# A new order of issue for the 2,740 hand-listed steps of a DeltaNet and MLP-mixer kernel

## The chip, the cores and the metric

The kernel runs on one core of one Trainium2 chip, in one launch. The time is that of the launch on the device, in microseconds (us); lower is better. A comparison of two kernels uses the medians of their runs.

## What is computed

The reference is a DeltaNet recurrence per batch and head, then an MLP-mixer (first over the tokens, then over the channels), all in float32:

```python
# q, k, v: (4, 8, 768, 48); beta: (4, 8, 768)
k_n = k / (np.linalg.norm(k, axis=-1, keepdims=True) + 1e-06)
state = zeros((B, H, D, D))
for t in range(S):
    kt, vt, bt = (k_n[:, :, t], v[:, :, t], beta[:, :, t, None])
    y[:, :, t] = np.einsum('bhd,bhde->bhe', q[:, :, t], state)
    v_old = np.einsum('bhde,bhd->bhe', state, kt)
    state = state + bt[:, :, :, None] * np.einsum('bhd,bhe->bhde', kt, vt - v_old)
# bridge: (B,H,S,D) -> x of (B, S, H*D) = (4, 768, 384)
xt = x.transpose(0, 2, 1)
h = np.maximum(xt @ w_tok1, 0.0) @ w_tok2      # 768 -> 256 -> 768
u = x + h.transpose(0, 2, 1)
h2 = np.maximum(u @ w_ch1, 0.0) @ w_ch2        # 384 -> 1536 -> 384
return u + h2
```

## The kernel before

The recurrence is done in chunks of 64 tokens. Inside a chunk the 64 updates are written as the inverse of a triangular 64 x 64 matrix, so that the tokens of a chunk are handled by matrix products and only the 48 x 48 state passes from chunk to chunk. There are 12 chunks in each of the 4 batches, so 48 steps of the recurrence, r0 to r47. Two chunks, 128 tokens of one batch with all eight heads, are a unit: 24 units, u = 0 to 23, six to a batch.

Everything is written as small Python generators ("jobs"). A job is called until its next `yield` and issues a few instructions each time; that is a step. The jobs, with the lines that matter here:

- `k{u}`, load_kq: the loads of k and q from HBM into pads (for early units) and kst (L403, four loads of 48 KB). `p{u}`, prep: squares of k (ksq, ScalarE, L465), their sum (VectorE, L468), the norm, the scaling, and the transposes of k and q into kq, by TensorE with a copy by ScalarE (L507, L511) for early units and by VectorE (L368) for units from 12 on.
- `c{u}` and `d{u}`, grams: for the first and the second chunk of a unit, the products of the transposed k with k and q (L442, p_g, two 64 x 128 products to a step), then a masking product on VectorE into gm.
- `t{u}`, to_parts, `i{n}`, invert, and `f{u}`, from_parts: 16 x 16 diagonal blocks are gathered from gm, inverted by VectorE (L655 to L687; seven rounds, i0 to i6) and put back. For the first six units the gathering is done by copies on three engines; for later ones four DMAs of a unit write the blocks to n_dram in HBM (L610), and four read them back (L635).
- `h{u}`, join_16, and `j{u}`, join: the inverses of 16 x 16 blocks are joined to those of 32 x 32 and 64 x 64 (L701 to L722, and L740 to L769: p_z L764, p_x L751).
- `v{u}`, load_v: four loads of v (L403, v_st, two buffers), then two scalings on GpSimd (POOL; L413, L416).
- `r{t}`, recur: one step of the recurrence: p_k (L804) from the state, rest (VectorE, L811), p_y and p_w (L824, L828), the copy w_t (ScalarE, L834), p_s (L842) and p_y (L843), the new state s_t (VectorE, L851 and L853), the output (ScalarE, L856).
- `m{b}`, mixer: the token and channel mixing of batch b in full 128 x 128 products (p L1000, p_h L1013, p_ut L1023, p_c L1080 for batch 0, p_r L972 for the others, p_o L1102, the addition L1031). Batch b's mixer fills TensorE while the recurrence of batch b + 1 goes on; m3 comes last, alone.
- `w{n}`, round_weights: a load of a piece of the mixer's weights into one of three buffers (L273, d64) and its rounding (ScalarE L279, VectorE L282, POOL L286). `s`, sum_weights (L913): sums of weights that the mixers need. `b`, load_beta. `x`, `z`, `Y`: products on zeros, with which TensorE is kept running while it has nothing else.

The matrix products of the recurrence and its preparation have at most 64 rows and 64 columns of the 128 x 128 array. Each uses one quarter of it: a row half (the partitions of its operands) and a column half (the partitions of its output).

The whole order of issue is one string of words, written out in the kernel (from L1176). A word is a job's name and `*n` for n steps in a row. A loop behind it takes them one after another:

```python
    for word in order.split():
        name, _, n = word.partition("*")
        for _ in range(int(n or 1)):
            next(jobs[name])
```

Each engine executes its own instructions in the order in which the string issues them. The DMAs here are issued by SyncE (SP), in order too: a DMA whose source is not ready holds up all those behind it. Buffers of a pool are given out in the order of allocation, so the string also decides which buffer a tile gets and whose last reader it has to wait for.

Of the kernel before, what the change touches and what calls it, by code (L numbers as in the profile page):

```python
# [23 lines left out]
def kernel(  # L24
# [149 lines left out]
    t11 = const.tile([128, NB, HB], FP32, name="t11")  # L174
# [18 lines left out]
    w1 = const.tile([128, NCH, DTOK], FP32, name="w1")  # L193
    w2 = const.tile([128, NDH, S], FP32, name="w2")
# [340 lines left out]
    t16 = spare[:, cuts[1] : cuts[2]].rearrange("s (q t b) -> s q t b", q=2, t=QB)  # L535
# [647 lines left out]
    c4*4 d4*2 w8 w6 i0*2 d4 z v0*2 i0*3 x k8 z*3 w1 i0*2 d4 x w17*3 t4 z h0*4 i0
    k5*2 h1*2 k8 h1*2 h0 h1 w17 z f0*3 h0 w8*2 p3 v1 h0 p5 f1*3 k8 h0*3 v1 v0 h0*2
    v0 h2*3 t4 h2 h0 z f2 h2 w0*2 j0 w11 j0 w6 j0*4 k5 h1*6 j0*3 h1*2 f2*2 j1 p5 t4
    v0 j0*2 w6 p5*6 h2 p5 r0 w14 h2*2 r0*4 h2*4 c5*4 k7 k9 h2 r0*2 p8 p5 j1 c5 j1*2
    r0 k7 r1*2 k7 k9 r1 k9 w0*2 r1 d5*3 r1 k9 w11*3 d5*2 j1 r1 w14 p6*2 w9 p8 v2 j1
    h3*2 t5 j2 r1 p6 h3*2 f3 r1 k9*2 h3 j1*2 w14 j1*3 k7 p6 t5*2 r1*2 r2*3 w9 r2 x
    j2*3 i1*2 w14 j2*2 p6 r2*2 w16 r2 p6 f3*2 h3 i1*4 k10 r2*2 h3 i1 h3 d6 h3 p6 r2
    r3*2 d6 r3 d6 r3 i1 v2 x i1 h3*4 r3 d6 v2*2 w16 c6*2 w9 c6*2 k10 d6 c6 p7 w16  # L1190
    p7 r3 j3 j2*2 r3 p7 r3*2 j2*2 j3 w9 j3 r4*2 k7 v3 p7 r4*2 j2 r3 j3*2 v2 j3 w16
    r4 k10 p7*2 w24 v3 r4*2 k10 i1*2 t6 i1 w5 p7*2 r4 w27 p7 j3*4 r4*2 d7 i1 r5 i1
    r5 i1 r5 j3 k8 v3*2 d7 r5*2 d7*3 k10 w5 c7*3 r5 w27 w5 v4 r5 w5 c7*2 r5 p8*3
    r5*2 r6*4 w24 v4 t7 i1 z p8*4 p9 v3 r6 h5 w27 h5 v4*2 h5*3 r6*2 w26 h4*2 t7 d8
    h4 w24 i1 h4*2 t7 d8*3 r6 w24 w27 t7 c8*4 t6*2 f4*3 d8 h4*3 p9 w26 p9 r6 r7 k10
    r7 r6 h4 p8 c8 w28 t6 h4*3 v4 r7*2 h4 w7 p9 r7 p9*2 r7 p9*2 r7*2 p9 c9 w26 w28
    j4 d9 c9 w26 k11 c9*2 f5 p10 w28*2 d9*3 r7 c9 r8*2 w7 t8*2 d9 r8*2 j4*2 p10 t8
    j4*2 w7 j4 p7 p10 t8 v5 m0 f5 p10 p9 f5 v5 j4*3 w4 w15 w4 r7 t9*2 w4 j4*2 t9*2
    h5 w15 z r8*2 h5*2 v5 h5 v5 r8*2 w27 w7 w4 w15 Y r8 r9*4 h5*3 r8 p10 h5 i2 j5*2
    r9*2 i2 w29 j5 p10*2 r9 j5 i2*3 j5 w29 w12 k11*2 k12 j5 r9 i2 k11 v7 m0 r9 w15  # L1200
    r10 j5*2 i2 j5 w12 w29 r10*2 i2 w19 i2 r10 p10 m0 p10 w19 k11*2 r9 v5 w12*2 k12
    d10*2 i2 w22 j5 d10 j5 r10*2 x i2 d10 i2 r10 w19 Y r10 i2*2 m0 w29 r10 w19 z
    w21 Y p11 k12 r11 r10 w31 Y i2 w22*2 r11*3 k12 i2*2 r11 i2 m0 r11 i2*2 w22 v7*2
    c10 w31 r11*2 c10*2 i2 k12*2 r11 m0 x i2*4 v7 k12 i2*4 x z w25 v6*2 m0 i2*2 v6
    k12*2 v6 k12 i2 f6 m0*2 c10 m0 f6*3 w25 m0 c10 m0 w21 w25*3 f7 m0*2 p11 w21*2
    w23 f7 m0*2 w27 d10 m0 p11 j6 v6 j6*4 p10 f7 w31*2 f7 w30 f8*3 p12 j6 j7 p12
# [92 lines left out]
```

## Time and profile before

| | before |
|---|---|
| median of 3 runs | 648.06 us |
| the runs | 646.71, 648.06, 651.08 us |
| span of the profiled execution, first to last instruction | 645.9 us |
| mean clock granted to TensorE | 0.987 |
| DMA traffic | 50.27 MB, mean 78 GB/s |

No other time of the profiled execution is known than its span. The profile's page lists for each engine its busy time; PE is TensorE's matrix products, PEld its weight loads, which run beside them; DVE is VectorE, ACT ScalarE, POOL GpSimd, SP SyncE. A line such as L842 is a line of the kernel's file. Rows of the waits and of the timeline name an instruction by engine, line, operation, and its tiles as output <- input; in brackets stands the idle time of the engine before it and what ended that. The page's overview over 40 slices of the span (busy share in tenths, granted clock in tenths, DMA rate in GB/s):

```profile
PE   8589888999999999999999999999999999999997
...
DVE  4986866978789756798977998585726353372643
ACT  7759767437412342223632423134326140232240
POOL 2437255224400221002100101010020000000000
PEclk8979979999999999999999999999999999999999
...
GB/s 185 166 126 130 164 147 180 158 104 139 112 88 80 89 105 74 95 89 100 93 71 125 58 78 42 63 17 50 5 44 4 25 3 0 25 1 25 1 26 25
```

One slice is 16.1 us. The costliest lines of the kernel are the full-size products of the mixers:

```profile
L1102 PE MATMUL p_o<-wc,r 128*128 128x192 f32 x720 | 126.3, 329 | 0.9 <-ACT u_t L1027 0.6
...
L1102 PE MATMUL p_o<-wc,s 128*128 128x192 f32 x288 | 51.2, 330 | 0.3 <-DVE xb L1031 0.3
...
L442 PE MATMUL p_g<-kq 48*64 48x128 f32 (+1 forms) x704 | 37.5, 285 | 7.8 <-ACT kq L511 6.2
```

The columns are the line, the engine, the operation with output and inputs, the count, then the busy time in us and the mean length of one in ns, then the idle time of the engine in front of them and what ended most of it.

### The profile page before, as it was taken

How to read it: one execution, taken by the hardware profiler on the slowest of the kernel's cores; microseconds unless marked ns; L12 is line 12 of the kernel's file. 1: busy time of each engine (PE TensorE's matmuls, PEld its weight loads, DVE VectorE, ACT ScalarE, POOL GpSimd, SP SyncE). 2: the span in 40 equal slices, each digit the busy share in tenths (PEclk: the TensorE clock that was granted, in tenths of full speed). 3: DMA queues.
4: the chain of work that ended last, by engine and by line, in shares of the span. 5: the costliest groups of instructions: out<-in, count | busy, mean ns of one | idle time of the engine just before them, and what ended most of it. 6: DMA issues, size and time to landing. Idle time of an engine off the chain costs nothing. (4 is left out here: it accounts for less than half of the span.)

```text
span 645.9 us, 21493 instructions
## 1 busy us (share of the span) xinstructions
PE 615.6 (95%) x9136; PEld 533.2 (83%) x9136; DVE 446.8 (69%) x1132; ACT 259.9 (40%) x631; POOL 109.0 (17%) x147
## 2 busy tenths in 40 slices
PE   8589888999999999999999999999999999999997
PEld 4457766668888987968989999769999987999997
DVE  4986866978789756798977998585726353372643
ACT  7759767437412342223632423134326140232240
POOL 2437255224400221002100101010020000000000
PEclk8979979999999999999999999999999999999999
DMA  9755666545533343344434222202010000000000
GB/s 185 166 126 130 164 147 180 158 104 139 112 88 80 89 105 74 95 89 100 93 71 125 58 78 42 63 17 50 5 44 4 25 3 0 25 1 25 1 26 25
DMA packets 135776, 50.27 MB, mean 78 GB/s; under 512 B 114656, under 2 KB 130144, under 8 KB 135680
## 3 DMA queue, kind: packets, MB, share of 16 engines
q1 hardware_dynamic: 135680, 48.89, 33.3%
q8 instruction: 72, 1.18, 0.8%
q14 instruction: 24, 0.20, 0.1%
HBM read 39.42 MB, written 9.44 MB: 76 GB/s over the span
## 5 line engine op out<-in xcount | busy, mean ns | idle before, releaser
L1102 PE MATMUL p_o<-wc,r 128*128 128x192 f32 x720 | 126.3, 329 | 0.9 <-ACT u_t L1027 0.6
L1102 PEld LDWEIGHTS p_o<-wc,r 128*128 128x128 f32 x720 | 116.7, 190 | 3.0 <-ACT u_t L1027 1.1
L984 DVE TENSOR_TENSOR r<-r,p_r 128x512 f32<-128x512 f32 x90 | 59.4, 684 | 39.1 <-PE p_r L972 36.7
L1031 DVE TENSOR_TENSOR xb<-xb,p_o 128x192 f32<-128x192 f32 x84 | 29.3, 350 | 52.9 <-PE p_o L1102 52.7
L981 ACT COPY r<-p_r 128x512 f32<-128x512 f32 x54 | 31.3, 584 | 85.6 <-PE p_r L972 78.3
L668 DVE TENSOR_TENSOR x<-x,sub 128x84 f32<-128x84 f32 (+24 forms) x178 | 58.9, 331 | 6.1
L663 DVE TENSOR_TENSOR sub<-x 128x84 f32<-128x84 f32 (+24 forms) x178 | 58.0, 326 | 7.4 <-DMA x<-n_dram 3.2
L1080 PE MATMUL p_c<-u_t,wc 128*128 128x256 f32 x216 | 51.3, 387 | 1.3 <-ACT r L1089 0.7
L1102 PE MATMUL p_o<-wc,s 128*128 128x192 f32 x288 | 51.2, 330 | 0.3 <-DVE xb L1031 0.3
L1102 PEld LDWEIGHTS p_o<-wc,s 128*128 128x128 f32 x288 | 46.8, 190 | 1.2 <-DVE xb L1031 0.6
L1080 PEld LDWEIGHTS p_c<-u_t,wc 128*128 128x128 f32 x216 | 39.6, 190 | 7.4 <-ACT r L1089 1.1
L416 POOL TENSOR_TENSOR v_st<-v_st,nrm 128x384 f32<-128x384 f32 x24 | 20.3, 847 | 146.9 <-DMA v_st<-in_v_dram 79.4
L442 PE MATMUL p_g<-kq 48*64 48x128 f32 (+1 forms) x704 | 37.5, 285 | 7.8 <-ACT kq L511 6.2
L988 ACT ACTIVATE r<-r 128x512 f32<-128x512 f32 x54 | 33.8, 631 | 25.4 <-DVE r L984 25.1
L499 POOL TENSOR_TENSOR mb<-mask_c,cs 128x512 f32<-128x512 f32 x20 | 21.0, 1048 | 128.7 <-DVE cs L478 102.6
L856 ACT ACTIVATE xb<-p_y 64x192 f32<-64x192 f32 x96 | 31.1, 324 | 23.8 <-PE p_y L843 16.0
L972 PE MATMUL p_r<-u_t,wc 128*128 128x128 f32 x288 | 38.6, 277 | 0.0
L972 PE MATMUL p_r<-t_d,wc 128*128 128x128 f32 x288 | 37.7, 281 | 0.0
L442 PEld LDWEIGHTS p_g<-kq 48*64 48x64 f32 (+1 forms) x704 | 26.8, 136 | 12.0 <-ACT kq L511 7.3
L834 ACT COPY w_t<-p_w 128x192 f32<-128x192 f32 x48 | 15.2, 318 | 51.6 <-PE p_w L828 50.7
L972 PEld LDWEIGHTS p_r<-u_t,wc 128*128 128x128 f32 x288 | 35.3, 192 | 0.3
L972 PEld LDWEIGHTS p_r<-t_d,wc 128*128 128x128 f32 x288 | 34.1, 191 | 1.1 <-DVE r L984 0.2
(176 smaller groups left out, 1252.8 us busy)
## 6 DMA issues: line engine op xcount, KB each, us to landing
d<-in_moe_w_ch_dram SPq DMA_DIRECT2D x24, 384.0 KB, 3.8
v_st<-in_v_dram SPq DMA_DIRECT2D x96, 48.0 KB, 2.4
out_dram<-xb SPq DMA_DIRECT2D x23, 192.0 KB, 1.9
kst<-in_k_dram SPq DMA_DIRECT2D x64, 48.0 KB, 2.7
n_dram<-gm SPq DMA_DIRECT2D x72, 32.0 KB, 1.8
pads<-in_k_dram SPq DMA_DIRECT2D x24, 96.0 KB, 2.6
pads<-in_q_dram SPq DMA_DIRECT2D x24, 96.0 KB, 3.2
gm<-w_dram SPq DMA_DIRECT2D x72, 32.0 KB, 2.1
```

The lines of the kernel that those rows point to most:

```text
L442: nc.tensor.matmul(p_g[PAR[i ^ cc], p], kqt[f, p, cc, 0], kqt[f, p, cc])
L499: scaler.tensor_tensor(out=mb, in0=mask_c[:, None, None, :].to_broadcast([128, NP, 2, C]), in1=cs[:, :, :, None].to_broadcast([128, NP, 2, ...
L663: nc.vector.tensor_tensor(out=tmp, in0=y[:, :, 0:s, s : s + 1].to_broadcast([n, k, s, w]), in1=y[:, :, s : s + 1, s + 1 : m].to_broadcast( ...
L668: nc.vector.tensor_tensor(out=y[:, :, 0:s, s + 1 : m], in0=y[:, :, 0:s, s + 1 : m], in1=tmp, op=ALU.add,)
L856: nc.scalar.mul(y[:, :, D * i : D * i + D], p_y[PAR[1 - i]], 1.0 if c else -1.0)
L972: nc.tensor.matmul(p[:, i], pieces[i // width][:, at : at + 128], f[f"u{n}"], start=first and i == 0, stop=True, skip_group_check=True,)
L981: nc.scalar.copy(o, p)
L984: nc.vector.tensor_tensor(out=o, in0=o, in1=p, op=ALU.add if sign > 0 else ALU.subtract)
L988: nc.scalar.activation(o, o, ACTF.Relu)
L1031: nc.vector.tensor_tensor(out=xb[:, c, e], in0=xb[:, c, e], in1=p, op=ALU.add)
L1080: nc.tensor.matmul(p_c[:, k], piece_of(wc1, cb, f * 128)[:, f * 128 : (f + 1) * 128], u_t[:, cb], start=(cb == 0), stop=(cb == NCB - 1),)
L1102: nc.tensor.matmul(p, a[:, m], wc2[:, m, j], start=(start and i == 0), stop=(i == NM - 1), skip_group_check=True,)
```

## The change

Only the string `order` is changed. Both strings have 2,740 steps and every name the same number of times, so every job issues the same instructions with the same operands in the same order within the job. How the jobs' steps are interleaved is new from the first line to the last; the new string is broken into 101 lines instead of 85 because it has fewer repetitions (`*n`). It comes from a search with a model fitted on the trace. In the string after the change every line number of the kernel above it is as before; lines below it are 16 higher.

The diff, cut to the start, the grams of u0 to u3, the place where w5, w27, w24 and t6 lie, the loads of k17, and the end:

```diff
     order = """
-    w10 z w10*2 z k1 z b k0 k1*2 b z x k1*2 k3 k0 z k1 k0*2 p1*2 k0 w2 k0 p0*2 b p1
-    p0 w10 p0*7 p1*3 k3*2 w2 d0 w2 c0 k2*2 c0 w18 d0*3 k3 w2 c0*3 d0 k3 p1*3 c1*2
-    p1 c1*3 k2*4 p2 d1 x d1*3 k3 t0 p2*2 w3 d1 p2*2 w13 p2*4 c2*2 d2 p2 p3*2 k4*3
...
-    c3 t2*2 t3*2 k7 p4 w1 t3 i0 p6 i0 p6*2 p4*2 i0*7 k8 z p4*4 v1 c4 k8 w6 d4 w1
...
-    r4 k10 p7*2 w24 v3 r4*2 k10 i1*2 t6 i1 w5 p7*2 r4 w27 p7 j3*4 r4*2 d7 i1 r5 i1
-    r5 i1 r5 j3 k8 v3*2 d7 r5*2 d7*3 k10 w5 c7*3 r5 w27 w5 v4 r5 w5 c7*2 r5 p8*3
...
-    p16 m0 r21*2 j12*2 k16 j12 f13 k17 r21 j12*2 p16 r22*4 m0*2 p15 v11 r22*3 p16
-    m0 k17*2 r22 k17*2 s*3 k17 r22*2 c16 d16 t15 c16 d16 f12 d16*3 c16 t15 r23 c16
-    t14*2 k17*2 r23*4 p17 m0 k17*3 r23 c16 p17*5 k17 p17 m0*4 s c17 v12 d17 c17*2
...
-    m2*2 r45 m2*3 r46*5 m2*5 j23 m2*12 r46*2 m2 r46*3 m2*4 r47*4 m2*4 r47*3 m2*6
-    r47 m2*5 m3*4 r47 m2*2 m3*2 m2 m3*7 m2*12 m3*2 m2 m3*159
+    w10 k1 k0 b k3 k1 w10 k1 k0 z k1*2 z w10 k0 w2 k0 z*2 k0*2 b w10 k2 k1 k3 p0 b
+    x v0 k3 w13 p0*3 p1 z p1 p0*5 p1 x w2 w3 k2 k4 w2 p1*2 d0 c0 d0 c0 d0 c0 v1 k2
+    p0 d0 p1 k2 d0 k2 c0 k2 c0 k4 p1 k5 k3 p1 k3 p1 d1 p2 w2 d1 c1 d1 p1 c1 d1 k3
+    c1 p2 c1 t0 p2 d1 p2*2 p3 c1 p2*2 k4 p2*3 w3 d2 w3 p3 c2 d2 w18 k6 k4 k6 t0
...
+    c3 d3 t1 p4 d3 t2 c3 w13 w1 d3 c3 d3 t1 w18 p4 c3 k5 p4 w18 t2 t3 w8 p4 t0 p6
+    x t3 p4 p6 t3 v1 t2 p4 i0 w1 i0*2 w1 i0 p4 x k5 i0 k6 w18 i0 p6 i0 p4*2 v0 w8
...
+    r3 p7 w5 j2 c6 v2 j2 k10 j3*2 r3 r4*2 p7 j3 i1 r4*3 j2 j3 p7 w16 v3 i1*2 r3 r4
+    v3 w27 i1 j3 p7 w24 p7 i1 p7 t6 r4*2 p7 r4 j3*4 d7 t6 r4 i1*2 r5*4 d7 j3 d7 c7
+    r5 w5 w27 d7 r5 c7 i1 w5 k10 c7 v3 r5 c7 r5 w5 k10 p8 d7 c7 p8 r5 z r6*2 r5
...
+    m0 r22 d16 m0 r22*2 c16 d16*2 s c16 r22 d16 c16 d16 r23 v12 k17 c16 r22 k17
+    p17 f13 k17*2 f12 c16 k17 r23*3 m0 r23 p17 r23 s p17 v12 s t14 p17 t16 v14
...
+    r46 m2*2 r46*2 m2*5 r46 m2*2 r46*2 m2*5 r47*5 m2*11 r47 m2 m3 m2 r47 m3*3
+    r47*2 m3*2 m2 m3*6 m2 m3 m2*4 m3 m2 m3*3 m2*6 m3*157
     """
```

Of the same name every step keeps its number: the first `w5` of the string is always the load, the later ones the rounding.

More of the change, by code (lines that the diff above doesn't have):

```diff
@@ L1183 @@
[L1183 to L1188, printed above, removed]
@@ L1195 @@
[L1195 to L1200, printed above, removed]
@@ L1201 @@
[L1201 to L1206, printed above, removed]
@@ new lines @@
+    w4 t9 j4 h5 p9 r8 w4 w7 p10 t9 h5 t9 w4 r8 t9 h5*2 Y r8 h5*2 w7 k12 p10 j5 r8
+    w15*2 w7 v5 r9 r8 i2*2 h5 i2 r9 i2 w12 r9 w12 r9 m0 r9 i2 p10 r9 j5 w12 j5 r9
+    w15 k11 i2 j5 w19 j5 i2*2 p10 w12 r9 k11 p10 v5 i2 m0 v7 j5 w19 p10 x w29 j5*2
+    k12*2 j5 r9 j5 v7 w29 k11 r10 i2 v5 w22 r9 r10 w29 k12 r10 i2 r10*2 m0 j5 i2
+    w19 r10 p10 w22 i2 r10 i2 Y d10 c10 d10 r10 v7 z r10 r11 Y w19 i2 r11 c10 w22
+    i2 r11 r10 r11*2 m0 i2 r11 k11 w22 d10 p11 r11 v6 Y c10 k12 v6 r11 v6 v7 r11
+    c10 k12 i2 d10 x i2 x i2*2 k12*2 v6 i2*4 w25 i2 m0 w29 m0 i2 m0 i2 w23 w21 i2
```

137 lines of the change are left out of this document (81 added, 56 removed).

## The prediction

> **What bounds the kernel now.** I read the busy line of the page first, then the busy time by stage, then the list of TensorE's waits, and last the timeline around the longest waits. The page:
>
> ```profile
> span 645.9 us, 21493 instructions
> ...
> PE 615.6 (95%) x9136; PEld 533.2 (83%) x9136; DVE 446.8 (69%) x1132; ACT 259.9 (40%) x631; POOL 109.0 (17%) x147
> ```
>
> TensorE (PE) is idle for 645.9 - 615.6 = 30.3 us in all, so nothing on another engine can be worth more than that unless it also makes TensorE's own work shorter. Where the 30.3 us lie is read from the stages; the columns are the stretch, its length, the busy time of each engine with its instructions, the clock granted to TensorE, the DMA share and GB/s:
>
> ```profile
> 0.00:43.00 43.00, 31.56 (x285) 19.65 (x286) 30.95 (x91) 27.87 (x70) 14.69 (x25) 0.88 0.91 172
> 43.00:112.00 69.00, 60.36 (x1714) 50.40 (x1715) 51.19 (x124) 54.75 (x150) 37.57 (x47) 0.95 0.62 146
> 112.00:250.00 138.00, 134.53 (x2193) 110.98 (x2193) 106.25 (x266) 52.88 (x136) 31.10 (x37) 1.00 0.45 108
> 250.00:400.00 150.00, 147.76 (x2265) 132.63 (x2265) 129.24 (x328) 53.80 (x130) 18.91 (x27) 1.00 0.38 85
> 400.00:528.00 128.00, 127.43 (x1924) 113.65 (x1923) 72.90 (x196) 43.37 (x102) 6.71 (x11) 1.00 0.12 27
> 528.00:646.00 118.00, 114.00 (x762) 105.93 (x760) 56.23 (x130) 27.24 (x48) 0.00 (x0) 1.00 0.04 14
> ```
>
> In the first 43 us TensorE lacks 11.4 us and much of its busy time is the filler products on zeros; it waits for loads and for the first inversion. From 43 to 112 us (the recurrence of the first batch, r0 to about r9) it lacks 8.6 us, and the clock of 0.95 costs 60.36 x 0.05 = 3.0 us more. From 112 us on it lacks 3.5 + 2.2 + 0.6 + 3.9 us in 534 us: there the time is TensorE's work, and an order can win only by the few waits left or by packing the products more tightly. Last come the longest waits by cause (total, times, longest):
>
> ```profile
> PE p_g L442 <- ACT kq L511: 6.2, 4, 3.8
> PE p_s L842 <- ACT w_t L834: 3.1, 5, 2.0
> PE p_t L507 <- DMA pads<-in_q_dram: 2.4, 1, 2.4
> PE p_y L843 <- issue: 1.6, 1, 1.6
> PE p_g L442 <- DVE kq L368: 1.5, 1, 1.5
> ```
>
> **The change, part by part.** Both orders have 2,740 steps, the same number of each name, so every engine gets the same instructions (4,652 matmuls, two records each). On TensorE and VectorE an instruction moves on average by under 1 us of its own engine's work, and the first p of m0 (L1000) has the same work ahead of it. So no stage moves as a whole. What moves is the neighbourhood of each step.
>
> *Before 43 us.* The first and third wait (6.2 and 2.4 us) lie here mostly. Their end is set by VectorE's inversion i0:
>
> ```profile
> 29.49 1.95 DVE L655 STREAM_TRANSPOSE x<-r 128x1024 f32<-128x1024 f32 x1
> 42.93 2.06 PE L701 MATMUL p_z<-r,wc 64*64 64x32 f32 x64 [0.40 <-DVE r L679]
> ```
>
> TensorE's next useful product (L701) comes when i0 is through. The new order loads k3, k4 and part of v0 and v1 earlier and moves the reduction of p6 (L468) ahead of i0's transpose; that should take the wait for L511 away, but TensorE would then only wait longer in front of L701. I count 0, from -1 (one step less inside i0) to +2 (a load of u0 to u3 pushed back by v0's).
>
> *From 43 to 112 us.* The 2.0 us wait for w_t is traced to the DMA queue:
>
> ```profile
> 74.33 2.35 SPq L610 DMA_DIRECT2D n_dram<-gm  x1
> 76.77 0.40 SPq L273 DMA_DIRECT2D d<-in_moe_w_tok_dram  x1
> 77.26 0.38 SPq L273 DMA_DIRECT2D d<-in_moe_w_ch_dram  x1
> ...
> 79.95 0.44 ACT L279 ACTIVATE d<-d 128x256 f32<-128x256 f32 x1 [1.05 <-DMA d<-in_moe_w_tok_dram]
> 81.15 0.55 ACT L279 ACTIVATE d<-d 128x384 f32<-128x384 f32 x1 [0.44 <-DMA d<-in_moe_w_ch_dram]
> 82.15 0.32 ACT L834 COPY w_t<-p_w 128x192 f32<-128x192 f32 x1
> 82.52 0.25 PE L842 MATMUL p_s<-w_t,gm 64*64 64x48 f32 x1 [2.01 <-ACT w_t L834]
> ```
>
> SyncE (SP) stood 2.35 us in t6's first write of n_dram, because its block was not ready; the loads of w5 and w27 came behind it, ScalarE waited 1.05 + 0.44 us for them, and the copy w_t of r5, queued behind, came late. In the new order w5, w27 and w24 are issued ahead of t6. ScalarE's queue is unchanged here (both roundings, then w_t), so its work still stands in front, but the 1.49 us of waiting should go: -1.5. That t6 is later costs nothing: its reader, inversion i2, starts far later. After this wait the clock fell:
>
> ```profile
> 83.00:85.00 2.00, 1.92 (x26) 1.42 (x21) 1.60 (x6) 1.23 (x4) 1.43 (x3) 0.54 0.45 83
> 85.00:88.00 3.00, 3.00 (x20) 1.77 (x17) 2.05 (x6) 1.49 (x3) 1.11 (x2) 0.50 0.80 177
> ```
>
> The stretch at about half clock is most of the 3.0 us above, and behind 112 us the stages show 1.00, although waits of 1.6 and 1.5 us lie there. So a wait cut from 2.0 to 0.5 us should not bring it about: I take -3.0, with 0 as the other bound, if the clock falls there all the same. The Trainium skill ("TensorE: Matmul & The Clock Gate", Part 1) says that the clock is either half or full and falls after an idle window of about 3.4 us whose phase runs freely; the 0.50 agrees, the length doesn't: 2.01 us of wait sufficed here. By that rule the remaining 0.5 us could not fill a window either, and the sum would be the same -7.8.
>
> *TensorE's packing.* The recurrence's and the preparation's products use a 64 x 64 quarter of the array each: rows of one half, outputs in the same half ("straight") or the other ("crossed"). A gram step of c is straight, of d crossed; p_z of a join is crossed, p_x straight; p_k is straight in even and crossed in odd steps. The trace shows what the neighbours are worth:
>
> ```profile
> 24.97 0.67 PE L442 MATMUL p_g<-kq 64*64 64x128 f32 x16
> 57.83 1.09 PE L442 MATMUL p_g<-kq 64*64 64x128 f32 x16
> ...
> 63.78 1.12 PE L764 MATMUL p_z<-t,gm 64*64 64x32 f32 x32
> 99.51 0.67 PE L804 MATMUL p_k<-s_t,kq 48*64 48x48 f32 x16
> ...
> 72.76:73.89 1.13, 1.13 (x48) 1.00 0.62 90
> ```
>
> The first sixteen records alternate c and d, the second sixteen are all d: 0.42 us for 8 matmuls, 0.053 us each. A p_z alone takes 1.12 and a p_k alone 0.67 us; where the two were interleaved (last row, 48 records) both took 1.13, so 0.66 us for 24 matmuls, 0.028 us each. I take 0.04. Counted in the two orders, the matmuls that stand in runs of eight or more of one kind fall from 431 to 373 ahead of the first p of m0 and from 385 to 293 behind it. Behind it, where TensorE is the bound: 92 x 0.04 = -3.7, between -2.6 and -4.9. Ahead of it 58 x 0.04 = -2.3, of which half may be lost in waits for the recurrence: -1.2.
>
> Against it stands that the finer order changes more often between full-size and quarter products, 93 times for 89. From the chain of waits:
>
> ```profile
> 517.30 1.98 PE p_r L972 x16
> ...
> 557.72 13.67 PE p_r L972 x120
> ```
>
> 120 in a row take 0.114 us each, so 16 take 1.82; with the change behind them they took 1.98. Four more cost 4 x 0.16 = +0.6, and twice that if the way back costs as much. The Trainium skill ("TensorEngine Tiling (Array Packing)", Key Properties) says that a change of tiling mode drains the engine, which speaks against such an order, and that tiles run independently; the trace agrees with both, at 0.16 us and at 0.42 us for 8 matmuls.
>
> *The wait for L368 at 254 us*, 1.5 us, likewise begins in the DMA queue:
>
> ```profile
> 243.62 2.46 SPq L610 DMA_DIRECT2D n_dram<-gm  x3
> 246.12 1.26 SPq L403 DMA_DIRECT2D kst<-in_k_dram  x2
> 249.84 0.52 ACT L465 ACTIVATE ksq<-kst 128x384 f32<-128x384 f32 x1 [4.04 <-DMA kst<-in_k_dram]
> 252.04 2.02 DVE L368 STREAM_TRANSPOSE kq<-pads 128x512 f32<-128x512 f32 x2
> 254.11 1.15 PE L442 MATMUL p_g<-kq 48*64 48x128 f32 x32 [1.54 <-DVE kq L368]
> ```
>
> The last two loads of unit 17's kst stood behind four writes of n_dram. In the new order the first three of the four stand ahead of one such write, the last behind it. With one write in front instead of four the last load can be about 2 us earlier, and the 1.54 us go: I count -1.0, between -1.5 and 0.
>
> *What the new order adds.* A reordering of 2,740 steps makes waits that this trace cannot show: steps that were late enough for their operands now come earlier. The row nearest is the wait of 2.01 us; I allow one such, +2.0, between 0 (the other engines' queues keep the same work ahead of TensorE's milestones) and three, +6.0.
>
> The sum: 0 - 1.5 - 3.0 - 3.7 - 1.2 + 0.6 - 1.0 + 2.0 = -7.8 us, a span of 638.1. The runs of before were 646.71, 648.06 and 651.08 us, their median 2.2 us above the span; the new time is then 640.3.
>
> **The rivals.** About 1% (6.5 us, outside 641.6 to 654.5) is what a measurement of this kernel can tell from no change.
>
> *Hidden anyway.* The quarter products saved lie under ScalarE's and VectorE's queues: from 43 to 112 us ScalarE is busy for 54.75 and VectorE for 51.19 of 69 us, and from 250 to 400 us VectorE for 129.24 of 150. Then only about half of the packing behind 112 us stays, -1.9, and one of the two DMA waits, -1.3, against +0.6 and +2.0: about 647.5. For it: the orders are near to each other. Against it: after 112 us TensorE lacks only 10 us.
>
> *Slower: w_t behind weight rounding.* ScalarE is in order; a copy w_t behind a rounding whose load is late costs what r5 paid, 2.0 us and a drop of up to 3.0. In the new order the copies of r10 and r11 also stand behind roundings (L279, L280). If each of r5, r10 and r11 paid 5.0 us where before only r5 did, the stage would be 10 us longer; with -3.7 + 0.6 + 2.0 from the rest this gives 657. It decides from two more such events on. Against it: the loads are earlier, not later, in the places I followed.
>
> *Not what it says.* The order also decides which buffer a load gets: v0 is now allocated ahead of v1, and the three d buffers go round in another sequence. A load that waits for a buffer blocks all of SyncE's queue; this would show as the rivals above, without a time of its own.
>
> *Much better.* All waits named go, the clock stays up and nothing new comes: -1.5 - 3.0 - 4.9 - 2.3 - 1.5 + 0.6 = -12.6, about 635.5.
>
> **How the numbers follow.** The forecast's mechanism has 0.58 (0.42 of it below 641.6, the rest between 641.6 and 645), hidden 0.22, much better 0.08, slower 0.12. The second part is the forecast with the clock falling all the same, 640.3 + 3.0 = 643.3. So faster by over 1%: 0.42 + 0.08 = 0.50; within 1%: 0.16 + 0.22 = 0.38; slower: 0.12. The range starts a little under the much better case, at 634. It ends at 651, where the hidden case has nearly its three new waits instead of one (647.5 + 4.0), and leaves out the slower case and an edge of the hidden one, together under 0.2.
>
> **What would show it.** Right: no wait of p_s for w_t near 82 us and no stretch at 0.50 clock after 80 us; L610 no longer ahead of w5 and w27 on SyncE; fewer than 30.3 us of idle; records of L442 and L804 in runs of the shorter kind, and TensorE's busy time down by 3 us or more. Wrong: busy time unchanged (packing was worth nothing), or a new wait over 1.5 us behind 112 us, above all on L368, w_t or rest.

## The result and the profile after

| | before | new order |
|---|---|---|
| median | 648.23 us (4 runs) | 666.89 us (4 runs) |
| runs | 646.71 to 651.08 us | 662.74 to 671.15 us |
| span of the profiled execution | 645.9 us | 660.9 us |
| granted clock, profiled execution | 0.987 | 0.982 |

The new order is slower: the ratio is 1.0318, with a 95% interval of 1.0268 to 1.0369. The prediction was 640.3 us with a range of 634 to 651; it had the sign wrong. The profiled execution is the fastest of the four, so its 15.0 us are the smallest of the runs' losses. The medians of the experiments leave out slow runs (1502 us in e10, 1000 us in e16, three of 650 to 657 us in e11 and e17), and of e10 and e16, whose profiled run was such a one, no profile is read.

The page of the new order:

```profile
span 660.9 us, 21502 instructions
...
PE 618.6 (94%) x9136; PEld 532.2 (81%) x9136; DVE 454.2 (69%) x1132; ACT 260.8 (39%) x631; POOL 110.8 (17%) x147
```

TensorE's busy time is 3.0 us longer and its idle time is 660.9 - 618.6 = 42.3 us instead of 30.3: 12.0 of the 15.0 us are new waits. The 3.0 us of busy time are about the clock: span times (1 - granted clock) is 11.9 us here and 8.4 us before. In the other three runs of the new order the clock was 0.972, 0.976 and 0.981, worth 12.6 to 18.7 us; in 13 runs of before beside the first experiments it was 0.984 to 0.995, worth 3 to 10 us. So of about 19 us in the median some 12 are waits and some 7 are lost clock (a run's time less its lost clock has a median of 652.2 us here and of 639.4 in those 13 runs).

The stages of the new order up to 400 us, with the same columns as in the prediction:

```profile
0.00:43.00 43.00, 29.13 (x280) 17.48 (x281) 32.69 (x89) 27.69 (x70) 14.93 (x27) 0.88 0.85 165
43.00:112.00 69.00, 60.35 (x1699) 48.60 (x1698) 53.04 (x126) 54.89 (x148) 36.24 (x44) 0.98 0.64 149
112.00:250.00 138.00, 130.11 (x2135) 106.68 (x2134) 105.16 (x259) 52.91 (x135) 31.78 (x38) 0.99 0.47 107
250.00:400.00 150.00, 142.41 (x2152) 125.77 (x2144) 119.87 (x306) 48.56 (x119) 18.62 (x24) 0.98 0.36 78
```

From 112 to 250 us TensorE now lacks 7.9 us (3.5 before) and from 250 to 400 us 7.6 us (2.2 before), with the clock at 0.99 and 0.98 where it was 1.00. These are the stages of which the prediction said that "the time is TensorE's work". The stage from 43 to 112 us, where it looked for most of the gain, has the same busy time as before and a better clock, 0.98 for 0.95.

Where the time went is seen best at equal work. The first p_k (L804) of a recurrence step has nearly the same products ahead of it on TensorE in both orders (up to r33, 1.4 us more or less at the steps shown). Its start, in us from the start of the span, read from the timelines:

| step | before | new order | later by |
|---|---|---|---|
| r1 | 57.23 | 58.61 | +1.4 |
| r13 | 152.84 | 152.73 | -0.1 |
| r18 | 201.61 | 204.03 | +2.4 |
| r23 | 245.76 | 250.55 | +4.8 |
| r27 | 298.69 | 306.63 | +7.9 |
| r29 | 311.62 | 323.38 | +11.8 |
| r33 | 352.54 | 366.72 | +14.2 |
| r47 | 519.21 | 536.03 | +16.8 (here some 2 us more work stand ahead of it) |
| end | 645.86 | 660.87 | +15.0 |

Against this execution of the kernel before, the head is not slower; all is lost between r13 and r33, most of it from r23 to r29. But the kernel before had itself lost some time ahead of r13 in this execution, which it does not in most others; that is shown under e7. The largest waits of TensorE in the new order (total, times, longest):

```profile
PE p_g L442 <- ACT kq L511: 6.9, 3, 5.0
PE p_o L1102 <- DVE xb L1031: 4.5, 4, 2.2
PE p_s L842 <- ACT w_t L834: 3.1, 6, 1.0
...
PE p_g L442 <- DVE kq L368: 2.3, 1, 2.3
```

The 2.0 us wait for w_t is gone (longest 1.0). New are the 4.5 us for the addition L1031, which were 0.5 before. Two of these waits, 2.3 us for L368 and 2.2 us for L1031, are longer than 1.5 us and lie behind 112 us: that is the prediction's own sign of being wrong. The timeline shows one of them, with SyncE and VectorE around it:

```profile
267.34 0.34 SPq L657 DMA_DIRECT2D x<-n_dram  x1
...
270.74 0.19 DVE L663 TENSOR_TENSOR sub<-x 128x30 f32<-128x30 f32 x1 [5.26 <-DMA x<-n_dram]
271.58 0.35 DVE L1031 TENSOR_TENSOR xb<-xb,p_o 128x192 f32<-128x192 f32 x1
271.98 2.22 PE L1102 MATMUL p_o<-wc,s 128*128 128x192 f32 x12 [2.16 <-DVE xb L1031]
...
281.28 0.36 SPq L1034 DMA_DIRECT2D out_dram<-xb  x1
```

The load of i4's blocks (L657) left SyncE at 267.34 us; in the old order it left at 260.53 us, though the new order is only 5 us late there. VectorE reached the first step of i4 (L663) and stood 5.26 us until the load landed. The addition that frees TensorE's PSUM buffer was queued behind it, so TensorE waited 2.16 us. Some 38 us later the first p_z of j14, which needs what i4 computed, waited 1.00 us for L740 and that for the read of w_dram, and the clock fell:

```profile
309.78 0.45 DVE L740 STREAM_TRANSPOSE t<-gm 128x256 f32<-128x256 f32 x1 [2.07 <-DMA gm<-w_dram]
...
310.28 0.30 PE L764 MATMUL p_z<-t,gm 64*64 64x32 f32 x2 [1.00 <-DVE t L740]
```

```profile
308.00:312.00 4.00, 2.65 (x67) 2.38 (x66) 2.22 (x4) 0.74 (x2) 0.00 (x0) 1.00 0.53 96
312.00:316.00 4.00, 3.79 (x69) 3.43 (x68) 2.10 (x5) 2.03 (x6) 2.99 (x3) 0.54 0.47 85
316.00:318.00 2.00, 2.00 (x79) 1.94 (x77) 1.19 (x4) 0.07 (x1) 0.00 (x0) 0.50 0.53 128
318.00:320.00 2.00, 2.00 (x14) 2.00 (x14) 1.97 (x4) 1.82 (x5) 0.00 (x0) 0.72 0.26 45
```

This wait and one of 0.35 us right behind it were followed by 8 us at about half clock, worth 4 x 0.46 + 2 x 0.50 + 2 x 0.28 = 3.4 us. The drop cost more than the waits.

### The profile page after: what moved, and what is told of

The parts are those of the page before. It is cut to its first block, busy times and chain, and to the rows that moved or that the text cites. A ratio compares the mean times of both kernels' runs of the same rounds, so it can differ in the third digit from the quotient of the medians.

```text
span 660.9 us, 21502 instructions
## 1 busy us (share of the span) xinstructions
PE 618.6 (94%) x9136; PEld 532.2 (81%) x9136; DVE 454.2 (69%) x1132; ACT 260.8 (39%) x631; POOL 110.8 (17%) x147
## 4 chain that ended last, share of the span: by engine, by line
PE 53%; DVE 15%; DMA 11%; SPq 8%; issue 8%; ACT 3%; POOL 1%; DVEq 0%; ACTq 0%; POOLq 0%
PE p_o L1102 17%; PE p_r L972 15%; DVE x L668 3%; DVE sub L663 3%; SPq L403 3%; PE p L1000 3%; PE p_c L1080 3%; PE p_h L1013 2%; DMA d<-in_moe_w_ch_dram 2%; PE p_k L804 2%; SPq L610 2%; SPq L635 2%; PE p_s L842 2%; DMA w_dram<-x 2%; PE p_y L824 2%
## 5 line engine op out<-in xcount | busy, mean ns | idle before, releaser
L1102 PE MATMUL p_o<-wc,r 128*128 128x192 f32 x720 | 129.4, 332 | 2.7 <-DVE xb L1031 2.1
L1031 DVE TENSOR_TENSOR xb<-xb,p_o 128x192 f32<-128x192 f32 x84 | 29.4, 350 | 61.2 <-PE p_o L1102 61.0
L981 ACT COPY r<-p_r 128x512 f32<-128x512 f32 x54 | 31.6, 585 | 99.2 <-PE p_r L972 99.1
L663 DVE TENSOR_TENSOR sub<-x 128x84 f32<-128x84 f32 (+24 forms) x178 | 59.5, 334 | 15.5 <-DMA x<-n_dram 11.9
L668 DVE TENSOR_TENSOR x<-x,sub 128x84 f32<-128x84 f32 (+24 forms) x178 | 65.7, 369 | 6.1
L442 PE MATMUL p_g<-kq 48*64 48x128 f32 (+1 forms) x704 | 38.9, 284 | 9.5 <-ACT kq L511 6.9
L856 ACT ACTIVATE xb<-p_y 64x192 f32<-64x192 f32 x96 | 31.1, 324 | 37.3 <-PE p_y L843 18.1
L972 PE MATMUL p_r<-t_d,wc 128*128 128x128 f32 x288 | 39.1, 288 | 0.0
L442 PEld LDWEIGHTS p_g<-kq 48*64 48x64 f32 (+1 forms) x704 | 26.6, 136 | 14.5 <-ACT kq L511 7.6
L972 PEld LDWEIGHTS p_r<-t_d,wc 128*128 128x128 f32 x288 | 35.5, 198 | 0.9
L286 POOL TENSOR_TENSOR wc<-w_f,d 128x384 uint32<-128x384 uint32 x24 | 26.0, 1086 | 60.8 <-ACT d L280 14.6
```

The lines of the kernel that those rows point to most:

```text
L286: nc.gpsimd.tensor_tensor(out=dst.bitcast(U32), in0=f, in1=lo, op=ALU.add)
L442: nc.tensor.matmul(p_g[PAR[i ^ cc], p], kqt[f, p, cc, 0], kqt[f, p, cc])
L663: nc.vector.tensor_tensor(out=tmp, in0=y[:, :, 0:s, s : s + 1].to_broadcast([n, k, s, w]), in1=y[:, :, s : s + 1, s + 1 : m].to_broadcast( ...
L668: nc.vector.tensor_tensor(out=y[:, :, 0:s, s + 1 : m], in0=y[:, :, 0:s, s + 1 : m], in1=tmp, op=ALU.add,)
L856: nc.scalar.mul(y[:, :, D * i : D * i + D], p_y[PAR[1 - i]], 1.0 if c else -1.0)
L972: nc.tensor.matmul(p[:, i], pieces[i // width][:, at : at + 128], f[f"u{n}"], start=first and i == 0, stop=True, skip_group_check=True,)
```

## The experiments

Each experiment ran beside kernels before on the same chip; their median was 645.8 to 647.3 us. A ratio is to those, with its 95% interval. The edits of the order are cut to the words where two strings begin to differ.

### Which half: the head or the tail

The two orders were joined at the first step of r12: the new order up to there and then the old one's remaining steps (first diff, against the new order), and the reverse (second diff, against the old one).

```diff
     j7*2 w25 k12 f8 m0 p11 w31
-    r12 p11 w23 w30 t10 r12 s r12 k12 r12*2 j8*2 w23
+    w30 w29 t10 w29 w23 p11 r12*3 p12 r12 f9 r12 w23
...
```

```diff
     j7*3 f8 m0 p11*3
-    r12*3 p12 r12 f9 r12 w23 j8*2 f9 w30 t10 w23
+    v7 r12*2 s r12 k12 r12*2 j8*2 w23*2 w32 j8
...
```

> The new order up to the first step of r12 (about 150 us), the old order behind it. In the profile of the change the same useful work of TensorE is done 0.4 us sooner than before at this point, and 15.3 us later at the end. If the loss is made where the traces show it (behind 160 us), this takes 646 to 649 us. Rival: the head leaves something behind (buffers in another sequence, queues further back) that the tail pays for; then over 655 us.

> The old order up to the first step of r12, the new one behind it. If the loss is made behind 160 us by the new order there, this takes 662 to 670 us. Rival (the head's state makes the loss): under 655 us.

The new head took 651.01 us (1.0071, 1.0032 to 1.0110), the new tail 659.34 us (1.0229, 1.0148 to 1.0310). The two losses add up to the whole. The tail makes most of it by itself, a little less than forecast; the head's 0.7% is more than its profile showed and was not expected. In the median run most of it is clock: the lost clock is 10.4 us in the runs of e1 and 7.1 in those of before, and the time without it 640.4 and 639.4 us.

### Transfers or computing steps

In e3 all steps that only issue a transfer on SyncE stand where the old order has them, among the computing steps of the new one, and in e4 the reverse. A few steps stand earlier or later than that where both orders agree on which of two comes first. In e6 only the transfers of one stretch were put back.

```diff
...
-    k1 k0 b k3 k1 w10 k1 k0 z k1*2 z w10 k0
+    w10 z k1 b k0 k1*4 z w10 z*2 k3
...
```

```diff
...
-    z w10*2 z k1 z b k0 k1*2 b z x k1
+    k1 k0 z w10*2 z*2 b k3 k1*2 k0 b z
...
```

```diff
     t9 h5*2 Y r8 h5*2 w7
-    k12 p10 j5 r8 w15*2 w7 v5 r9 r8 i2*2 h5 i2
+    p10 j5 r8 w15*2 w7 v5 r9 r8 i2*2 h5 i2 r9
...
```

> The new order for all computing steps, but the steps that only issue a transfer on SyncE (loads of k, q, v and weights, writes to n_dram, reads of w_dram) stand where the old order has them. Theory A, the new waits come from the order of the transfers on SyncE's queue: most of the loss goes, 648 to 655 us. Rival B, they come from the order of the computing steps on VectorE, ScalarE and TensorE: it stays, 661 to 670 us.

> The old order for all computing steps, the transfers on SyncE where the new order has them. Theory A (the transfers' order): 657 to 668 us. Rival B (the computing steps' order): 646 to 651 us. Between these, both have a part.

> The new order, but the transfers of the stretch before the first d13 product (k12 to k15, v8, v9, t10 to t13 and five loads of weights) stand where the old order has them. Theory: the wait of 2.3 us for L368 at 175 us comes from the load of q of u13 queued behind writes of n_dram and loads of v; with its stretch at lower clock it makes 4.2 us of the loss, so this takes 3 to 5 us less than the new order (661 to 664 us) and that wait is under 0.5 us. Rival: the lateness is in the computing steps, no change, 665 to 669 us.

e3 took 664.62 us (1.0321, 1.0234 to 1.0409), no better than the new order; e4 took 683.11 us (1.0559, 1.0490 to 1.0628), far worse than either order; e6 took 675.21 us (1.0440, 1.0378 to 1.0501). Neither theory held. Theory A expected e3 to be quick, theory B expected e4 to be. In e4 and e6 transfers out of step with the computing steps cost much more than either order does: in e6 one p_z alone waited 5.7 us for L740. In e3, which mixes the same two orders, they do not. That buffers freed late are the reason is likely, but was not traced. So the transfers cannot be judged apart from the computing steps, and these runs say nothing of which of the two makes the new order's loss.

### The inversion i4 and the stores behind it

In e5 only i4 and the transfers just ahead of it were put back to their old places. SyncE stood long in front of a store of the output (L1034): 11.9 us up to 281.28 us, as above. So e10, e11 and e12 issue the stores on GpSimd's queue: in the new order, in the old one as a control, and in e5.

```diff
     m0*8
-    f13 m0 p15 r18 d14*2 c14 d14 r18*2 f10 m0 p15 d14
+    m0 p15 r18 d14*2 c14 d14 r18*2 f10 m0 p15 d14 p15
...
```

```diff
-            nc.sync.dma_start(out=out[b, c * 128 : (c + 1) * 128, e], in_=xb[:, c, e])
+            nc.gpsimd.dma_start(out=out[b, c * 128 : (c + 1) * 128, e], in_=xb[:, c, e])
```

> The new order, but the inversion i4 (its load of n_dram, its 30 steps on VectorE, its write of w_dram) and the transfers just ahead of it (n_dram of t14 to t17, k18, v12, v14) stand where the old order has them. In the profile of the change i4 starts and ends some 4 us of TensorE's work later than before; two additions L1031 queue behind it on VectorE (waits of 2.2 and 1.3 us at 272 and 278 us) and the first p_z of j14 waits for its result at 311 us (1.4 us and a stretch at half clock). Theory: these two places make 3.8 + 4.8 us of the loss, so this takes about 8 us less than the new order: 655 to 660 us, and the three waits are under 0.3 us. Rival (the lateness is only seen there, its cause lies elsewhere and shows up at the next product): over 663 us.

> The new order, with the stores of the output (L1034) issued on GpSimd's queue instead of SyncE's. In the profile of the change SyncE stands 11.9 us in front of one store of m0 (269 to 281 us) and 24 us in front of those between 340 and 400 us, with loads of k and v and reads of w_dram behind them; before it stood 2.7 and 13.8 us there. Theory: this is what makes the loads behind late in the new order; without it the loss between 270 and 400 us (10 of 15 us in the profile) goes down by 4 us or more, to 658 to 663 us. Rival (what the loads wait for behind the stores holds them up all the same): 665 to 669 us.

> The control: the kernel before with the same edit. If the stores block nothing that matters in the old order, no change beyond 2 us either way (645 to 649 us).

> Both: the inversion i4 and its transfers as in the old order, and the stores on GpSimd's queue. Moving i4 back alone took away the waits of 2.2, 1.3 and 1.4 us, but a wait of 3 us at 306 us and one of 2.5 us at 333 us came in their place, and SyncE stood 9.4 us in front of a store there. Theory: the two causes are one behind the other, and both edits together give 652 to 658 us. Rival: still over 663 us.

e5 took 667.09 us (1.0301, 1.0245 to 1.0357): the same as the new order, as the rival said. TensorE's waits of e5 over the stretch, in the same columns as above:

```profile
PE p_r L972 <- ACT r L981: 1.7, 1, 1.7
PE p_x L751 <- DMA gm<-w_dram: 1.1, 1, 1.1
PE p_w L828 <- DVE rest L811: 1.1, 1, 1.1
PE p_k L804 <- DVE s_t L851: 1.0, 2, 0.8
```

The waits for L1031 and for L740 are gone, as the theory wanted, but others of about the same sum came: at r29 e5 is 9.9 us late where the new order is 11.8, and at r33 14.5 where it is 14.2.

e10 took 668.86 us (1.0355, 1.0294 to 1.0415), e12 675.29 us (1.0440, 1.0402 to 1.0479), and the control e11 646.28 us (0.9966, 0.9928 to 1.0003). The stores' theory got nothing out of this, but the test was not clean, as GpSimd's waits in e12 show:

```profile
POOL out_dram L1034 <- DVE sub L663: 62.8, 6, 22.7
POOL mb L499 <- DVE gm L445: 41.8, 4, 22.7
```

GpSimd now stood up to 22.7 us in front of a store whose addition stood behind an inversion (L663), and its scalings for the recurrence and the preparation behind it. In e12 the block was moved, not removed. Whether SyncE's wait at the store costs the new order anything stays open; stores merely issued later on SyncE were not tried.

### The clock

In e9 20 filler products (the expectation counts 21) stand directly ahead of ten products that wait in the new order's profile. One of the ten places:

```diff
     m1*3
+    z
     j14 r27
```

> The new order with 21 products on zeros (the kernel's own x and z steps, 0.2 and 0.85 us each) put into TensorE's queue directly ahead of ten products that wait in the profile of the change, so that TensorE is busy during the wait. It computes the same. Theory: a large part of the new order's loss, about 7 of 20 us in the median (lost clock 12 to 19 us a run against 3 to 10 before), is the clock falling behind waits of 1 to 2 us; with the waits filled the lost clock goes down to 6 to 10 us and the time to 658 to 662 us. Rival (the falls have nothing to do with these waits, and the fillers only add work): 667 to 672 us with the clock as before.

It took 667.62 us (1.0313, 1.0254 to 1.0373), no change. The clock was 0.980 to 0.987 in its four runs against 0.972 to 0.982 in the new order's, so the lost clock went down, from a median of 14.3 us to 10.0. What was left of the time went up by about as much, from 652.2 to 657.1 us (medians of a run's time less its lost clock). With four runs of each, that speaks for the first half of the theory, that the clock falls behind these waits; but the fillers pay for it with their own time: the products on zeros of L227 take 37.3 us in its profile and 25.9 in the new order's.

### Two terms of the forecast by themselves

e7 is the kernel before with a single step moved, t6's first write of n_dram, from ahead of the loads of w5 and w27 to behind them:

```diff
-    r4 k10 p7*2 w24 v3 r4*2 k10 i1*2 t6 i1 w5 p7*2 r4 w27 p7 j3*4 r4*2 d7 i1 r5 i1
+    r4 k10 p7*2 w24 v3 r4*2 k10 i1*3 w5 p7*2 r4 w27 t6 p7 j3*4 r4*2 d7 i1 r5 i1
```

> The kernel before with one step moved: the first write of n_dram (first t6) is issued behind the loads of w5 and w27 instead of ahead of them. The prediction's second term by itself: -1.5 us, and -3.0 us more in the runs where the clock falls there. The recurrence at r5 should wait under 0.7 us. In the chip's runs of before the lost clock was 3 to 10 us, so the fall may not come in each: 642 to 646 us where before takes 646. Rival (ScalarE's roundings in front of w_t set the wait, not the loads): no change.

It took 645.99 us (0.9992, 0.9962 to 1.0022): no change. The wait at r5 is 1.35 us, not under 0.7. All the same its profile seems to show the gain. The writes and loads now leave one behind the other, at 75.19, 75.83 and 76.26 us, ScalarE waits 0.39 + 0.43 us for the loads and no longer 1.05 + 0.44, its copy w_t starts at 80.53 us instead of 82.15, and the first p_k of r13 starts at 148.71 us, 4.1 us sooner than before.

But the moved step is not what makes this gain. Six other kernels of this document have the old order up to r12 or further, with t6 ahead of w5 and w27 (e2, e11, e15, e17, e18 and e19). In the profile of each of them SyncE is 0.55 us at t6's first write where it was 2.35 us, p_s waits 0.5 to 1.4 us for w_t where it waited 2.01, and r13 starts 0.7 to 3.2 us sooner than in the profile of before. In four of the six the clock is 1.00 from 78 to 92 us, where it was 0.76. The rows of e11, whose whole order is the old one:

```profile
74.03 0.55 SPq L610 DMA_DIRECT2D n_dram<-gm  x1
...
81.12 0.25 PE L842 MATMUL p_s<-w_t,gm 64*64 64x48 f32 x1 [0.77 <-ACT w_t L834]
```

So the 2.01 us at r5 and the fall of the clock behind them were an event of the one execution that was profiled, and not a fixed cost of the old order. Nor was the block late that the write of 2.35 us takes. The last products of unit 6 were masked into gm by 71.62 us, and the write began at 74.33:

```profile
70.34 1.28 DVE L445 TENSOR_TENSOR gm<-p_g,mb 128x512 f32<-128x512 f32 x2
```

What held that write up stays open.

The lead of e7 does not last, either: the first p_k of r27 is only 2.8 us ahead, that of r33 0.9 us. One place where it went:

```profile
251.35 1.15 PE L442 MATMUL p_g<-kq 48*64 48x128 f32 x32 [2.44 <-DVE kq L368]
```

It is the wait that took 1.54 us before, at 254.11 us. TensorE came 3.7 us sooner, VectorE's transpose only 2.8 us sooner. The smaller lead of e11, 2.2 us at r13, is still 1.7 us at r33.

e13 is the kernel before with the ten gram steps of each unit sorted, so that all of c come ahead of all of d:

```diff
     p0*2 p1*3 k3*2 w2
-    d0 w2 c0 k2*2 c0 w18 d0*3 k3 w2 c0*2
+    c0 w2 c0 k2*2 c0 w18 c0*2 d0 k3 w2 d0*2
...
```

> The kernel before with the ten gram steps of each unit in the order c, c, c, c, c, d, d, d, d, d, in the same places of the string. The matmuls in runs of eight or more of one kind rise from 385 to 626 behind the first p of m0 and from 431 to 503 ahead of it. The prediction's price of 0.04 us each gives +9.6 us behind it and up to +2.9 ahead: 652 to 660 us, and TensorE's busy time up by 8 us or more. Rival (outside a stretch with nothing else the order of the quarters is worth little): busy time up by under 3 us, 645 to 650 us.

It took 653.48 us (1.0103, 1.0056 to 1.0150), and TensorE's busy time rose by 6.8 us, to 622.4.

The gram products L442 themselves, by shape (count, then busy time in us and mean ns of one), in e13 and below it in the new order:

```profile
L442 PE MATMUL p_g<-kq 48*64 48x128 f32 x384 | 23.1, 276 | 0.9 <-DVE kq L368 0.9
L442 PE MATMUL p_g<-kq 64*64 64x128 f32 x320 | 22.3, 291 | 6.5 <-ACT kq L511 6.5
L442 PE MATMUL p_g<-wc 64*64 64x128 f32 x64 | 3.6, 277 | 1.0 <-ACT wc L511 1.0
```

```profile
L442 PE MATMUL p_g<-kq 64*64 64x128 f32 x320 | 19.6, 291 | 7.2 <-ACT kq L511 6.9 <-DVE gm L445 0.3
L442 PE MATMUL p_g<-kq 48*64 48x128 f32 x384 | 19.3, 278 | 2.4 <-DVE kq L368 2.3
L442 PE MATMUL p_g<-wc 64*64 64x128 f32 x64 | 2.3, 276 | 2.6 <-ACT wc L511 2.6
```

Sorted they take 49.0 us; the same lines took 17.7 + 19.8 + 3.1 = 40.6 us before. 313 more matmuls in long runs of one kind cost 8.4 us, 0.027 us each. The effect is real, at two thirds of the price taken. But the new order has 41.2 us: its finer alternation won nothing. Its quarter products as a whole (L442 to L843 of the grams, the joins and the recurrence) are busy for 271.6 us, added up by line, where they were for 265.5; a part of that is the lower clock.

### One stretch of the new order

All steps between the starts of r23 and r29 were exchanged: the old stretch in the new order (e14), the new stretch in the old order (e15), and the stretch from r12 to r18 of the new order in the old one (e16).

```diff
     d16*2 s c16 r22 d16 c16 d16
-    r23 v12 k17 c16 r22 k17 p17 f13 k17*2 f12 c16 k17 r23
+    p16 s*2 r22 f12 r23 c16 t14*2 k17 r23*4
...
```

```diff
     c16 d16 f12 d16*3 c16 t15
-    r23 c16 t14*2 k17*2 r23*4 p17 m0 k17*2
+    v12 k17 r23 v12 k17 c16 k17 p17 f13 k17*2 c16 k17 r23
...
```

```diff
     j7*3 f8 m0 p11*3
-    r12*3 p12 r12 f9 r12 w23 j8*2 f9 w30 t10 w23
+    v7 r12*2 s r12 k12 r12*2 j8*2 w23*2 w32 j8
...
```

> The new order, but all steps between the start of r23 and the start of r29 as in the old order. Over this stretch the new order loses 7 us of the 15 in its profile (from 5.1 to 12.1 us late at equal work of TensorE). If the stretch makes its own loss: 7 to 10 us less than the new order, 656 to 661 us. If the loss is carried over from queues that are late already, or comes back behind the stretch: over 664 us.

> The old order, but all steps between the start of r23 and the start of r29 as in the new one. If the stretch makes its own loss: 5 to 9 us more than before, 651 to 656 us. If it needs the lateness from ahead: within 2 us of before, 645 to 649 us.

> The old order, but all steps between the start of r12 and the start of r18 as in the new one. In the profile of the change this stretch loses 4 us (0.2 us late at its start, 4 us at its end; the wait for L368 at 175 us). If it makes its own loss: 3 to 6 us more than before, 649 to 653 us. If the old order behind it takes the loss up, or the wait is carried over from the new head: within 2 us, 645 to 649 us.

e15 took 654.39 us (1.0145, 1.0078 to 1.0212): the stretch makes its own loss, in an order that is not late. Against before its first p_k of r23 is 2.0 us early, of r27 2.4 us late, of r29 4.8 and of r33 5.7 us late, and it stays there to the end. e16 took 647.85 us (1.0042, 1.0000 to 1.0084): little or nothing is made between r12 and r18. e14 took 664.68 us (1.0290, 1.0213 to 1.0368): inside the old stretch no time is lost (4.7 us late at r23, 3.5 at r29), but at r33 it is 11.1 us late. The loss comes back right behind the seam, where the new order's queues meet the old stretch's, in waits of p_s for w_t (1.6 us the longest) and of p_r for L981 (1.1 us). Part of that may be the seam itself, as in e3 and e4; the run cannot tell.

### The parts of the stretch

In the old order, only the 32 steps of i4 stand as in the new one (e17; some stand up to 10 places earlier, the last up to 13 later); only the transfers of the stretch (e18); only its computing steps, i4 among them (e19). In e18 and e19 some steps of the other kind moved with them.

```diff
     m0 j13 m0*2 t17*4
-    i4*5 j13*4 k18*3 i4*2
+    j13*2 i4*3 j13*2 i4 k18*3 m0*2 i4
...
```

```diff
     c16 d16 f12 d16*3 c16 t15
-    r23 c16 t14*2 k17*2 r23*4 p17 m0 k17*2
+    v12 k17 r23 v12 k17 c16 k17 r23*4 p17 f13 k17
...
```

```diff
     c16 t15 r23 c16 t14*2 k17*2
-    r23*4 p17 m0 k17*3 r23 c16 p17*3
+    p17 r23*3 m0 k17*3 c16 r23 p17 r23 p17*2
...
```

> The old order with one part of the stretch from r23 to r29 as the new one has it: only the 32 steps of the inversion i4, of which the last stand 9 to 13 steps later. The stretch as a whole costs 8 us. If the late inversion is its cause (the first p_z of j14 waits for it, and the clock falls there): 3 to 5 us more than before, 649 to 651 us, with a wait of over 1 us at L764. Rival: nothing, 645 to 648 us.

> The old order with only the transfers of the stretch from r23 to r29 (k18 to k20, v12 to v14, n_dram of t14 to t17, reads of w_dram) where the new one has them. If the transfers' places by themselves are the cause: 651 to 656 us. If they cost only together with, or are made worse without, the computing steps that they were chosen for: over 656 us. If they are not the cause: 645 to 648 us.

> The old order with only the computing steps of the stretch from r23 to r29 in the new order, the transfers where the old one has them. If the computing steps are the cause: 651 to 656 us. If the transfers are: 645 to 648 us. If only their fit counts, this and the run with the transfers alone are both slower than before by 3 us or more.

e17 took 650.84 us (1.0086, 1.0046 to 1.0127), e18 650.90 us (1.0071, 1.0037 to 1.0105) and e19 648.08 us (1.0037, 0.9998 to 1.0077), where the stretch as a whole costs 1.0145. No part is the cause alone. The transfers and the computing steps, which together are the stretch, cost 0.71% and 0.37%; their sum of 1.1% lies within the interval of the whole, 0.8 to 2.1%. The late inversion alone costs 5 us, as its theory said, but not at the place it named: the first p_z waits for no more than 0.6 us. With the stretch's other computing steps in their new places too, both together cost 2 us or nothing. How it costs is seen on two queues. The first is VectorE's; e17, then the same place before:

```profile
270.52 0.35 DVE L1031 TENSOR_TENSOR xb<-xb,p_o 128x192 f32<-128x192 f32 x1
270.79 0.37 DVE L663 TENSOR_TENSOR sub<-x 128x210 f32<-128x210 f32 x1
...
276.53 0.41 DVE L668 TENSOR_TENSOR x<-x,sub 128x240 f32<-128x240 f32 x1
276.86 0.61 DVE L1031 TENSOR_TENSOR xb<-xb,p_o 128x192 f32<-128x192 f32 x2
...
277.26 2.20 PE L1000 MATMUL p<-xb,w 128*128 128x384 f32 x6 [2.75 <-DVE xb L1031]
```

```profile
271.70 0.35 DVE L1031 TENSOR_TENSOR xb<-xb,p_o 128x192 f32<-128x192 f32 x1
...
275.39 0.35 DVE L1031 TENSOR_TENSOR xb<-xb,p_o 128x192 f32<-128x192 f32 x1
...
277.30 0.35 DVE L1031 TENSOR_TENSOR xb<-xb,p_o 128x192 f32<-128x192 f32 x1
```

In e17 seven pairs of i4 (the widths 210 to 240) stand between two additions, 6.3 us from start to start, and TensorE, which needs the PSUM buffer that the addition empties, waits 2.75 us. In the old order the additions come every 2 to 4 us there and no product waits for one. The work on VectorE is the same; where the additions stand in it is not.

The second queue is SyncE's. i4 ends later, so the store of its result (L687) leaves SyncE at 294.39 us instead of 291.05, the ten reads of it (L635) from 298.92 instead of 294.06, and the loads of kst behind them from 310.17 instead of 306.80. ScalarE's square ksq waits for such a load, VectorE's sum L468 for ksq, and rest, which stands behind that sum on VectorE, comes too late for p_w. In the old order VectorE waits 0.42 us in front of that sum, and no product waits for rest there. From e17:

```profile
315.48 0.52 ACT L465 ACTIVATE ksq<-kst 128x384 f32<-128x384 f32 x1 [3.00 <-DMA kst<-in_k_dram]
316.04 0.55 DVE L468 TENSOR_REDUCE ksum<-ksq 128x8 f32<-128x384 f32 x1 [2.42 <-ACT ksq L465]
...
317.50 0.25 PE L828 MATMUL p_w<-rest,gm 64*64 64x48 f32 x1 [1.85 <-DVE rest L811]
```

These two waits, 2.75 and 1.85 us, are most of the 5.7 us that e17's profile loses against before's from r23 to r33.

## Why the prediction was wrong

**The step that failed** is "What the new order adds": "I allow one such, +2.0, between 0 (the other engines' queues keep the same work ahead of TensorE's milestones) and three, +6.0". That term was taken at +2.0 us and measured some 19: TensorE's idle time grew by 12.0 us in the quickest run although the waits at r5 and at 254 us went away, and in the median run some 7 us of lost clock come on top. The bound rested on counts of work ahead of a few milestones and on a mean displacement of under 1 us of an engine's own work. e17 shows what that average hides: 32 steps moved by 13 places at most, no work added, 5 us, through waits on the queues of VectorE and SyncE. e15 shows that a stretch of the new order makes 8 us by itself where nothing was late before it.

**Before 43 us**: forecast 0, with the wait for L511 gone and the time lost again ahead of L701. The wait for L511 was not taken away (6.9 us for 6.2, the longest 5.0 for 3.8), so the reason was wrong. The first p_k of r1 came 1.4 us later, inside the range of -1 to +2, but by luck.

**The wait at r5**, -1.5 and -3.0, a second step that failed. The row of SyncE's queue was read rightly, but its reason was not (the block was ready 2.7 us before), and the wait and the fall of the clock were priced as the old order's own, from one execution. In the six other profiles with the old order at this place the wait is 0.5 to 1.4 us. Across this place, from 74 to 94 us, TensorE gains 3.0 us in the new order against the profile of before (from 1.9 us late to 1.1 early at equal work: products done, each at its line's mean length, without the fillers). In four of those six, where no step was moved there, it gains 3.7 to 4.3 us (2.1 and -0.2 in the other two). So the new order won nothing here that other executions of the old one do not have, and the 4.5 us were not there to be won in the median: e7, with the step moved, ends where the kernel before does. The clock of e7 still fell, to 0.68 from 83 to 88 us.

**The packing**: -3.7 and -1.2 from 0.04 us for each matmul no longer in a long run. e13 shows the price, 0.027 us for grams, so the mechanism is right and its size half again too high. The new order nevertheless has 41.2 us of gram products where 40.6 stood before. So the count of runs of eight or more did not foretell the time of this order. That shorter groups between full-size products take the gain back is likely, but was only argued, here and in the term of +0.6 for the switches, which no run measured alone.

**The wait for L368 at 254 us**: forecast -1.0; it is gone in the new order, and TensorE gains 1.6 us across the place at equal work. The same kind of wait, 2.3 us, stands at 175 us instead.

**The rivals.** The slower one, w_t behind weight roundings at r5, r10 and r11, did not happen: the waits for w_t are 3.1 us in total in both profiles. "Hidden anyway" is near to e7, whose lead shrank, but e7's lead was mostly not its edit's. The case that came, other queues stopping at waits of their own and the clock falling behind them, had a chance of 0.12 under another mechanism's name. The prediction's trust in 534 us of stages where "TensorE lacks only 10 us" was misplaced: that a stage has no waits in one order says nothing of another order.

**What stays open**: which of the new order's steps make the rest. The tail makes 13 us, and the stretch from r23 to r29 makes 8 of them alone. Of these the two waits of e17 are traced step by step; the transfers' 5 us (e18) are not, and neither are the 5 us of the tail outside the stretch. The head makes 5 us in the median, most of it clock. Not one of these orders was quicker than the kernel before.

## What to carry to other kernels

When a hand-made or searched order hides its waits, an engine that is 95% busy is no proof that only its own work counts: follow for each in-order queue what stands between two instructions that the busy engine waits for (here the pairs of an inversion between two additions, and a late store ahead of loads). Price a new order's unknown waits by more than the longest wait of the old one. Before a wait is priced as something to win, look for it in a second profile: the 2.0 us at r5 stood in one of seven. Transfers and computing steps moved apart from each other can cost far more than either order (e4, e6), though over one stretch each alone cost less than both.

## What the runs showed of the hardware that was not expected

Some of VectorE's small products and sums in the inversion take up to four times as long when an elementwise instruction of GpSimd begins at about the same time. The new order has one at 436.70 us; the rows are from its timeline:

```profile
435.83 0.40 DVE L668 TENSOR_TENSOR x<-x,sub 64x238 f32<-64x238 f32 x1
...
436.69 0.83 POOL L416 TENSOR_TENSOR v_st<-v_st,nrm 128x384 f32<-128x384 f32 x1 [30.33 <-DVE sub L663]
436.70 1.08 DVE L668 TENSOR_TENSOR x<-x,sub 64x240 f32<-64x240 f32 x1
```

The sum of 64 x 240 took 1.08 us where its neighbour of 64 x 238 took 0.40. In the profile of the new order 41 instructions of VectorE are more than 0.15 us over the median of their line and shape, and all 41 overlap one of GpSimd; before there are 31, all of them too. Not every overlap costs: 29 more of L663 and L668 overlap one of GpSimd in the new order and stay under that bound. The difference lies in the inversion's L663 and L668, whose lines together are busy for 125.2 us instead of 116.9. VectorE's busy time as a whole grew by 7.4 us, from the order alone. The Trainium skill ("GPSIMD Engine Reference", Specifications) says that GpSimd shares its SBUF interfaces with VectorE and contends with instructions that have two SBUF inputs, as L663 and L668 do; the trace agrees, at 1.08 us for 0.40. What it costs the kernel was not measured by itself.
